# Moving normalisations, gate multiplies and residual adds from VectorE to GpSimd in a gated long-convolution block

## The chip, the cores and the metric

The kernel runs on one core of a Trainium2 chip. The core has five engines with a queue each: TensorE (PE in the profile; PEld is its weight load), VectorE (DVE), ScalarE (ACT), GpSimd (POOL) and SyncE (SP). Each engine works through its own queue in order, and semaphores hold an instruction until what it needs is done. The metric is the device time of one execution in microseconds; a version is judged by the median of its runs.

## The reference

The input x has 2048 positions of 640 channels, in bfloat16. It is normalised per position, and two branches are multiplied and added to it:

```python
xn = _layernorm(x, axis=-1)
# branch s: a 4-tap shift filter over k, times v, then a causal convolution
# of length 2048 per channel (by FFT of length 4096), plus a direct term, times xn
kv = k_shift * v
y = irfft(rfft(kv_pad) * rfft(kf_pad))[:S] + kv * ssm_D
s = xn * y
# branch g: a two-layer network on xn
g = _silu(_gelu(xn @ w1 + b1) @ w2 + b2)
return x + s * g
```

The hidden layer of the network is 1728 wide.

## The kernel before, in words

**Tiling.** 128 partitions hold 16 positions each, so a "row" n2 (0 to 15) is a tile of 128 x 640. Four rows make a chunk; the input lies in four tiles `xn_tiles`, one for each chunk c (0 to 3; the text counts chunks 1 to 4). A tile holds first x, then the normalised x, then that times the gate, and for the last chunk also the result.

**The network.** For each chunk: statistics (`ln_stats`, steps `ls`), the reciprocal root of the variance on GpSimd (`ln_eps`, `ln_root`; `lv`, `lr`), the normalisation of one row (`ln_norm`, `ln4` to `ln15`, line 361; the first chunk is normalised in the prologue by other code), transposes on TensorE (`tt`) and their copies to SBUF (`te`), the first layer (`h` on TensorE, line 377; `he` on ScalarE, line 383), the second layer by halves of a row (`g0` to `g31`, line 396), its silu on ScalarE into a buffer `sl` (`ge0` to `ge31`, line 401), and the multiplication of that into the normalised row (`ffn2_mul`, `gm0` to `gm31`, line 406). Chunk c has gates 8c to 8c + 7. The `sl` buffers are two: a silu can start only when the gate multiply of the buffer's last user is done. The second layer's PSUM tiles are two as well (`ps_ffn`).

**The convolution.** It is done as matrix multiplications in two factors. The filter: transposes (`kt`, `kc`), first factor (`kf`, evacuated by `ke` on ScalarE when the step ends in `.a`, on VectorE for `.d`), stores to a scratch in DRAM (`ks`, issued by GpSimd, line 437), reloads (`fl`), second factor (`ff`, `fe`). The input: shift filter and product on VectorE (`cv`, lines 467 to 473), first factor (`uf`, `ue`), stores by GpSimd (`us`, line 447), reloads issued by SyncE (`ml`, line 513), second factor (`mu`, line 521), products with the filter (`mp`, line 526), first inverse factor (`mc`, `me`), stores by GpSimd (`ms`, line 541), reloads (`yl`, line 547). A reload of either scratch takes one line out of every store, so it needs all sixteen stores. The stores' SBUF source is a ring of four pairs of rows (`pools["ring"]`). The PSUM tiles of this branch are three (`ps_big`).

**The end.** The second inverse factor (`inv2`, steps `y`, lines 553 and 554) gives a row in PSUM; `gate` (`yt`, line 560) multiplies it with the gated row. For the first three chunks the product goes to one of two `row` buffers `t1`; `out_add` (`yo`, line 564) adds the input to it and writes half of a pair `o` in a ring of two pairs (`pools["store"]`); when both rows of a pair are there, GpSimd issues its store (`out_store`, `ys`, line 568). The input is loaded a second time by chunks (`xq_load`, steps `q0` to `q3`, line 544) into two `quad` buffers, so the load for chunk 3 waits until the adds of chunk 1 are done, and that for chunk 4 until those of chunk 2 are done. For the last chunk the order is other: product first, then gate (`gm24` to `gm31`), then the add (`last_add`, `ga`, line 411) and the store by SyncE (`last_store`, `gs`).

**The order.** It is written out by hand in `PLAN`, a list of steps which the kernel issues one by one; each engine gets its instructions in this order. So an instruction that moves to another engine keeps its place in `PLAN` and takes the corresponding place in that engine's queue, between what the plan has before and after it there. GpSimd's queue before holds a few constants, three `lr`, and the stores `ks`, `us`, `ms` and `ys`.

Of the kernel before, what the change touches and what calls it, by code (L numbers as in the profile page):

```python
# [14 lines left out]
ALU = mybir.AluOpType  # L15
# [59 lines left out]
def kernel(  # L75
# [15 lines left out]
    nc = tc.nc  # L91

    CH = 4
# [218 lines left out]
    live = {}  # L312
    pools = {}

    def take(key, pool, shape, dtype, tag, bufs=None):
        if key not in live:
            live[key] = pool.tile(shape, dtype, tag=tag, name="%s%d" % key, **({"bufs": bufs} if bufs else {}))
        return live[key]
# [39 lines left out]
    def ln_norm(i):  # L358
        c, j = divmod(i, CH)
        xr = xn_tiles[c][:, j, :]  # L360
        nc.vector.tensor_scalar(out=xr, in0=xr, scalar1=live["mv", c][:, j, 0:1], scalar2=live["rs", c][:, j:j + 1],
                                op0=ALU.subtract, op1=ALU.mult)

    def x_tr(i):
# [21 lines left out]
    def ffn2_at(i):  # L386
        c, r = divmod(i, 2 * CH)
        q, h = divmod(r, 2)
        return c, q, slice(h * HALF, (h + 1) * HALF)
# [13 lines left out]
    def ffn2_mul(i):  # L403
        c, q, hs = ffn2_at(i)
        xr = xn_tiles[c][:, q, hs]
        nc.vector.tensor_tensor(out=xr, in0=xr, in1=live["sl", i][:], op=ALU.mult)  # L406

    def last_add(i):
        c, q, hs = ffn2_at(i)
# [151 lines left out]

    def out_add(n2):
        o_sb = take(("o", n2 // 2), pools["store"], None, None, None)
        nc.vector.tensor_tensor(out=o_sb[:, n2 % 2, :], in0=live["t1", n2][:], in1=live["xq", n2 // CH][:, n2 % CH, :],
                                op=ALU.add)

    def out_store(i):
        nc.gpsimd.dma_start(out=out_v[:, 2 * i:2 * i + 2, :], in_=live["o", i])
# [1 line left out]
    def prologue():  # L570
# [89 lines left out]
    steps = {  # L660
        "P": load_params, "pt": param_tr, "pb": param_out, "X": load_x, "A": load_w1, "B": load_w2, "C": load_kf, "K": load_k, "V": load_v,
        "ls": ln_stats, "lv": ln_eps, "lr": ln_root, "ln": ln_norm, "tt": x_tr, "te": x_tr_out,
        "h": ffn1, "he": ffn1_out, "g": ffn2, "ge": ffn2_silu, "gm": ffn2_mul, "ga": last_add, "gs": last_store,
        "w": f1_phase, "ws": f1_sines, "d": add_d, "em": tap3, "ee": tap3_out,
        "sp": small_iotas, "s": small_phase, "ss": small_sine, "sm": small_mats,
        "kt": k_tr, "kc": k_tr_out, "kf": k_f1, "ke": k_f1_out, "ks": k_store,
        "cv": kv_step, "uf": u_f1, "ue": u_f1_out, "us": u_store,
        "fl": kin_load, "ff": k_f2, "fe": k_f2_out, "it": i2_tr, "ie": i2_out,
        "ml": uin_load, "mk": swap_load, "mu": u_f2, "mp": product, "mc": inv1, "me": inv1_out, "ms": c_store,
        "q": xq_load, "yl": cab_load, "y": inv2, "yt": gate, "yo": out_add, "ys": out_store,  # L670
    }
    with tc.manual_schedule():
        prologue()
        for step in PLAN.split():
            kind, at, eng = re.fullmatch(r"([A-Za-z]+)(\d*)(?:\.(\w))?", step).groups()
# [31 lines left out]
```

## Time and profile before

| | us |
|---|---|
| median of 3 runs | 229.04 |
| lowest and highest run | 227.22, 229.06 |
| span of the profiled execution | 225.2 |
| median less that span | 3.84 |
| busy, TensorE / VectorE / ScalarE / GpSimd | 209.3 / 183.2 / 149.7 / 42.5 |

The profile gives the profiled execution's own time as its span, from the first instruction to the last; what lies around the span in that execution it doesn't give, and the timed runs stand 2.0 to 3.9 us above it. Rows of the timeline begin with the start and the duration in us, then engine, line, operation, output and inputs, and how many were merged; in brackets stands the idle time of the engine before it and what ended it. Rows by line give the number of instructions, the busy time in us and the mean of one in ns. Rows of the chain give the start, the length on the chain, and what it was. Rows by stage give each engine's busy time between two moments.

### The profile page before, as it was taken

To read this page: it belongs to the slowest core of one execution; us is meant where nothing else is said; L and a number is where in the kernel's file an instruction comes from. 1 tells how busy PE (TensorE), PEld (TensorE's weight loads), DVE (VectorE), ACT (ScalarE), POOL (GpSimd) and SP (SyncE) were. 2 spreads that over 40 slices of the span, in tenths; PEclk is the share of its full clock that TensorE was granted. 3 is DMA by queue.
4 is the path that set the end of the run, shared out by engine and by line. 5 is a ranking of instruction groups with operands and counts; after the bars stand their busy time and mean duration, and the time that the engine had idled before them with its cause. 6 is when DMAs were issued, how large, how long until landed. Compare 5 with 4: busy or idle time off the path is not lost.

```text
span 225.2 us, 3912 instructions
## 1 busy us (share of the span) xinstructions
PE 209.3 (93%) x1420; PEld 131.5 (58%) x1420; DVE 183.2 (81%) x309; ACT 149.7 (66%) x232; POOL 42.5 (19%) x72
## 2 busy tenths in 40 slices
PE   7869989899999899979999988999999999999993
PEld 4624457677555556645765544565777755457771
DVE  7799999989989999999859998999996125445792
ACT  3946697998988999999549665576762263671111
POOL 8000011032232345030200221203222000100010
PEclk9999999999999999999999999999999999999999
DMA  6999996645844469599849999866833694389223
GB/s 215 347 381 357 406 410 277 218 193 198 303 186 189 178 209 388 185 320 324 320 167 286 335 399 361 273 231 254 273 118 140 215 367 153 119 260 388 80 92 116
DMA packets 25209, 57.61 MB, mean 256 GB/s; under 512 B 2854, under 2 KB 14055, under 8 KB 25190
## 3 DMA queue, kind: packets, MB, share of 16 engines
q1 hardware_dynamic: 20726, 39.66, 50.7%
q0 software_dynamic: 4320, 17.70, 20.6%
q8 instruction: 11, 0.18, 0.3%
q14 instruction: 8, 0.07, 0.1%
q10 hardware_dynamic: 144, 0.01, 0.0%
HBM read 33.76 MB, written 18.35 MB: 231 GB/s over the span
## 4 chain that ended last, share of the span: by engine, by line
PE 59%; issue 13%; ACT 11%; DVE 7%; DMA 7%; SPq 1%; POOL 1%; DVEq 0%; POOLq 0%; ACTq 0%
PE g L396 20%; PE h L377 20%; ACT Khat L135 5%; DMA prm<-in_B_b_dram 4%; PE uf L337 3%; PE mc L534 2%; DMA scrC<-c 2%; PE mc L535 2%; PE kf L337 2%; PE mu L337 2%; PE y L553 2%; PE y L554 2%; DVE p L526 2%; DVE Khat L136 2%; PE ff L337 1%
## 5 line engine op out<-in xcount | busy, mean ns | idle before, releaser
L377 PE MATMUL h<-xnT,w_sb 128*128 128x512 bf16 x280 | 65.8, 379 | 1.3 <-ACT hT L383 1.0
L396 PE MATMUL g<-w_sb,hT 128*128 128x320 bf16 x448 | 63.7, 299 | 0.6 <-ACT sl L401 0.6
L396 PEld LDWEIGHTS <-hT 128*128 128x128 bf16 x448 | 43.8, 98 | 18.1 <-issue 0.8
L383 ACT ACTIVATE hT<-h,b_f 128x512 bf16<-128x512 f32 (+1 forms) x56 | 38.3, 690 | 23.2 <-PE h L377 20.7
L526 DVE TENSOR_TENSOR p<-mu,Khat 128x1280 bf16<-128x1280 f32 x32 | 45.8, 1484 | 3.1 <-PE mu L337 2.1
L377 PEld LDWEIGHTS <-w_sb 128*128 128x128 bf16 x280 | 27.3, 98 | 29.3 <-issue 1.5
L401 ACT ACTIVATE sl<-g 128x320 bf16<-128x320 f32 x32 | 14.0, 439 | 36.1 <-PE g L396 32.5
L135 ACT CAST c<-mc 128x640 bf16<-128x640 f32 x29 | 19.9, 692 | 6.5 <-PE mc L535 5.7
L541 POOL DMA_DIRECT2D scrC<-c x16 | 11.5, 718 | 51.9 <-ACT c L135 47.7
L406 DVE TENSOR_TENSOR xn<-xn,sl 128x320 bf16<-128x320 bf16 x32 | 10.0, 320 | 13.7 <-ACT sl L401 13.5
L469 DVE TENSOR_TENSOR uc<-uc,kvtmp 128x1280 bf16<-128x1280 bf16 x24 | 19.8, 824 | 0.7
L473 DVE TENSOR_TENSOR kvtmp<-kh,w_exp 128x1280 bf16<-128x1280 bf16 x24 | 19.7, 819 | 0.5
L534 PE MATMUL mc<-p,mats 128*128 128x320 bf16 x64 | 18.1, 298 | 1.6 <-DVE p L526 1.1
L560 DVE TENSOR_TENSOR t<-y,xn 128x640 bf16<-128x640 f32 x12 | 9.8, 820 | 10.6 <-PE y L554 10.5
L337 PEld LDWEIGHTS <-mats 128*128 128x128 bf16 x128 | 12.0, 97 | 10.8 <-issue 3.8
L535 PE MATMUL mc<-p,mats 128*128 128x320 bf16 x64 | 18.1, 298 | 0.0
L135 ACT CAST Khat<-uf 128x640 bf16<-128x640 f32 x26 | 17.0, 697 | 0.4 <-PE uf L337 0.4
L135 ACT CAST Khat<-ff 128x640 bf16<-128x640 f32 x24 | 15.5, 699 | 0.5 <-PE ff L337 0.4
L135 ACT CAST Khat<-kf 128x640 bf16<-128x640 f32 x22 | 15.1, 711 | 0.3 <-PE kf L337 0.2
L437 POOL DMA_DIRECT2D scrK<-Khat x16 | 8.9, 554 | 29.7 <-ACT Khat L135 16.6
L337 PE MATMUL mu<-kh,mats 128*128 128x320 bf16 x64 | 13.6, 298 | 0.8 <-DMA kh<-scrU 0.4
L337 PE MATMUL ff<-kin,mats 128*128 128x320 bf16 x64 | 12.3, 298 | 1.3 <-ACT Khat L135 1.3
(111 smaller groups left out, 269.0 us busy)
## 6 DMA issues: line engine op xcount, KB each, us to landing
scrK<-Khat POOLq DMA_DIRECT2D x16, 320.0 KB, 2.5
scrU<-Khat POOLq DMA_DIRECT2D x16, 320.0 KB, 4.3
kin<-scrK SPq DMA_DIRECT2D x16, 320.0 KB, 4.9
Khat<-Khat SPq DMA_DIRECT2D x32, 160.0 KB, 3.8
kh<-scrU SPq DMA_DIRECT2D x16, 320.0 KB, 5.2
scrC<-c POOLq DMA_DIRECT2D x16, 320.0 KB, 3.6
kh<-scrC SPq DMA_DIRECT2D x16, 320.0 KB, 6.0
kh<-in_A_k_dram SPq DMA_DIRECT2D x4, 640.0 KB, 5.9
```

What stands on the lines that cost most here:

```text
L135: return nc.scalar.copy(out=out_ap, in_=in_ap)
L337: nc.tensor.matmul(out=ps[:, h, 0:HALF], lhsT=lhsT, rhs=rhs[:, h * HALF:(h + 1) * HALF], start=start, stop=stop)
L377: nc.tensor.matmul(out=ps[:, :], lhsT=w1_sb[:, t, ft * P:(ft + 1) * P], rhs=xnT[:, t, :], start=(t == 0), stop=(t == DT - 1))
L383: nc.scalar.activation(out=hT[0:M, ft, :], in_=live["h", i][0:M, :], func=ACT.Gelu_apprx_tanh, bias=b1_f[0:M, ft:ft + 1], scale=1.0)
L396: nc.tensor.matmul(out=ps[:, 0:HALF], lhsT=hT[0:M, ft, q * P:(q + 1) * P], rhs=w2_sb[0:M, ft, hs], start=(ft == 0), stop=(ft == FT - 1))
L401: nc.scalar.activation(out=sl[:], in_=live["g", i][:, 0:HALF], func=ACT.Silu)
L469: nc.vector.tensor_tensor(out=uc[:], in0=uc[:], in1=kvtmp[:], op=ALU.add)
L473: nc.vector.tensor_tensor(out=(kvtmp if s else uc)[:], in0=kh[:, r0:r0 + KC, :], in1=w_exp[:, j:j + 1, :].to_broadcast([P, KC, D]), op=ALU ...
L526: nc.vector.tensor_tensor(out=p[:].rearrange("p k (h c) -> p k h c", h=2), in0=live["mu", g][:, None, :, 0:HALF].to_broadcast([P, 2, 2, HA ...
L534: nc.tensor.matmul(out=psC[:, h, 0:HALF], lhsT=I1a, rhs=p[:, 0, hs], start=True, stop=False)
L535: nc.tensor.matmul(out=psC[:, h, 0:HALF], lhsT=I1b, rhs=p[:, 1, hs], start=False, stop=True)
L541: nc.gpsimd.dma_start(out=pair_view(scrC)[g2], in_=live["c", g2][:])
```

## The change

Three operations are issued on GpSimd instead of VectorE: the normalisation of the rows of chunks 2 to 4 (twelve instructions of 128 x 640), the gate multiplies of chunks 1 to 3 (24 of the 32, of 128 x 320), and the addition of the input for rows 0 to 7 (eight of 128 x 640; the rows 8 to 11 stay, and so do the last chunk's own adds). `PLAN`, the buffers and everything else stay as they are.

```diff
     def ln_norm(i):
         c, j = divmod(i, CH)
         xr = xn_tiles[c][:, j, :]
-        nc.vector.tensor_scalar(out=xr, in0=xr, scalar1=live["mv", c][:, j, 0:1], scalar2=live["rs", c][:, j:j + 1],
+        nc.gpsimd.tensor_scalar(out=xr, in0=xr, scalar1=live["mv", c][:, j, 0:1], scalar2=live["rs", c][:, j:j + 1],
                                 op0=ALU.subtract, op1=ALU.mult)
...
     def ffn2_mul(i):
         c, q, hs = ffn2_at(i)
         xr = xn_tiles[c][:, q, hs]
-        nc.vector.tensor_tensor(out=xr, in0=xr, in1=live["sl", i][:], op=ALU.mult)
+        eng = nc.gpsimd if i < 24 else nc.vector
+        eng.tensor_tensor(out=xr, in0=xr, in1=live["sl", i][:], op=ALU.mult)
...
     def out_add(n2):
         o_sb = take(("o", n2 // 2), pools["store"], None, None, None)
-        nc.vector.tensor_tensor(out=o_sb[:, n2 % 2, :], in0=live["t1", n2][:], in1=live["xq", n2 // CH][:, n2 % CH, :],
-                                op=ALU.add)
+        eng = nc.gpsimd if n2 < 8 else nc.vector
+        eng.tensor_tensor(out=o_sb[:, n2 % 2, :], in0=live["t1", n2][:], in1=live["xq", n2 // CH][:, n2 % CH, :],
+                          op=ALU.add)
```

## The prediction

> **What bounds the kernel now.** I read the page first: busy shares, then the chain that ended last.
>
> ```profile
> span 225.2 us, 3912 instructions
> PE 209.3 (93%) x1420; PEld 131.5 (58%) x1420; DVE 183.2 (81%) x309; ACT 149.7 (66%) x232; POOL 42.5 (19%) x72
> PE 59%; issue 13%; ACT 11%; DVE 7%; DMA 7%; SPq 1%; POOL 1%; DVEq 0%; POOLq 0%; ACTq 0%
> ```
>
> TensorE is busy for 93% of the span and holds 59% of the chain; VectorE, busy for 81%, holds 7%. So VectorE's work is full of pieces that end while TensorE or ScalarE is later still, and taking work off VectorE is worth only what lies in those 7%. Then I read the busy time by stage, from the start of chunk 2's normalisation to the end of chunk 2's gates, the stretch in which most of the moved work lies:
>
> ```profile
> core 0: us, PE busy (x) PEld busy (x) DVE busy (x) ACT busy (x) POOL busy (x), PEclk, DMA share, GB/s
> 28.00:118.00 90.00, 84.61 (x617) 55.96 (x615) 83.29 (x155) 78.24 (x124) 22.25 (x35) 1.00 0.70 254
> 183.00:214.00 31.00, 31.00 (x190) 18.46 (x189) 16.47 (x29) 13.65 (x20) 2.19 (x4) 1.00 0.61 217
> ```
>
> From 28 to 118 all three compute engines are nearly full (TensorE idle for 5.4 of 90 us, VectorE for 6.7), each in its fixed order: a delay on any of them reaches the others. From 183 to 214 TensorE has no idle time at all, so nothing there can be won, only lost.
>
> **What moves, and its price.** Rows by line and form:
>
> ```profile
> L406 DVE TENSOR_TENSOR xn<-xn,sl 128x320 bf16<-128x320 bf16 x32 | 10.0, 320 | 13.7 <-ACT sl L401 13.5
> L361 DVE TENSOR_SCALAR xn<-xn,mv,rs 128x640 bf16<-128x640 bf16 x12 | 4.9, 439 | 0.0
> L564 DVE TENSOR_TENSOR w_exp<-t,xq 128x640 bf16<-128x640 bf16 x12 | 5.6, 490 | 2.5 <-DMA xq<-in_A_q_dram 2.2
> L356 POOL TENSOR_TENSOR rs<-ve,mhalf 128x4 f32<-128x4 f32 x3 | 4.5, 1513 | 28.4 <-DVE ve L352 28.4
> masks.py:199 POOL TENSOR_SCALAR_AFFINE_SELECT ident<-ident 128x128 bf16<-128x128 bf16 x1 | 0.3, 295 | 0.1
> L230 POOL IOTA GB<- 128x128 f32 x1 | 0.2, 243 | 0.0
> L229 POOL IOTA GB<- 128x16 f32 x1 | 0.1, 145 | 0.0
> ```
>
> VectorE gives up 24 of the 32 gate multiplies (24 x 0.320 = 7.7 us), 12 normalisations (12 x 0.439 = 5.3) and 8 of the 12 final adds counted here (8 x 0.490 = 3.9). What each costs on GpSimd no row shows. From below: no faster than on VectorE (0.32, 0.44, 0.49); nothing excludes that. From above: the only GpSimd row that reads two tensors takes 1.51 us, a power on 4 elements; I use it as a high end of 1.5 for a multiply and, with the per-element part below, 2.9 for an add. Between them, by the small GpSimd rows: two iotas differ by 112 elements and 98 ns, 0.875 ns per element written and 131 ns fixed; the select reads and writes 128 elements in 295 ns, (295 - 131) / 128 = 1.28 ns; a second operand, taken at the cost of one more pass, makes 2.16 ns. So a normalisation is 0.131 + 640 x 1.28 ns = 0.95 us, a gate multiply 0.131 + 320 x 2.16 ns = 0.82, an add 0.131 + 640 x 2.16 ns = 1.51. These estimates I take, being from rows with real streaming in them.
>
> [...]
>
> **Loss A: the first stores (43 to 49 us).** GpSimd also issues the stores of the first transform, in plan order `ke1.d ks0 gm2 ge4 ln6 kf3 ke3.d ks1 kf4 ke4.a gm4 ge5`. The silu outputs have two buffers, held by the second and third gates, so ge4 must wait for gm2 and ge5 for gm4.
>
> ```profile
> 43.83 0.32 DVE L406 TENSOR_TENSOR xn<-xn,sl 128x320 bf16<-128x320 bf16 x1
> 44.06 0.44 DVE L361 TENSOR_SCALAR xn<-xn,mv,rs 128x640 bf16<-128x640 bf16 x1
> 45.18 0.32 DVE L406 TENSOR_TENSOR xn<-xn,sl 128x320 bf16<-128x320 bf16 x1
> 44.53 0.73 POOL L437 DMA_DIRECT2D scrK<-Khat  x1 [10.00 <-DVE xn L361]
> 45.83 0.55 POOL L437 DMA_DIRECT2D scrK<-Khat  x1 [0.57 <-ACT Khat L135]
> 44.68 0.46 ACT L401 ACTIVATE sl<-g 128x320 bf16<-128x320 f32 x1
> 45.59 0.48 ACT L401 ACTIVATE sl<-g 128x320 bf16<-128x320 f32 x1
> 44.80 0.34 ACT sl L401
> 45.73 0.34 ACT sl L401
> ```
>
> Now gm2 (43.83) runs beside the store; afterwards it stands behind it. Store to 45.26, gm2 to 46.08, ge4 at 46.1 instead of 44.68; ln6 to 47.03, the second store (0.55) to 47.58, gm4 to 48.4, ge5 at 48.4 instead of 45.59: 2.8 us. If the first store starts as soon as its data is there, some 0.6 earlier, it is 2.2; I take 2.5. The last two rows are from the chain: both silus stand on it, and behind them in ScalarE's order stand the evacuations for which TensorE waits, so nothing hides this. The transposes of chunk 2 (TensorE at 45.6) wait for ln6 too, but less. Lower end 1.4 (VectorE's durations), upper end 5. The three normalisations and two gates before 43 us come no later than now: GpSimd is idle from 34.5 to 44.5.
>
> **Loss B: the last scratch store (110 us).** gm12 and gm10 stand on GpSimd ahead of the last two stores of the input's transform; the reload waits for all of them.
>
> ```profile
> 109.77 0.54 POOL L447 DMA_DIRECT2D scrU<-Khat  x1 [0.74 <-ACT Khat L135]
> 114.53 0.88 SPq L513 DMA_DIRECT2D kh<-scrU  x2
> 117.50 0.43 PE L337 MATMUL mu<-kh,mats 128*128 128x320 bf16 x2
> ```
>
> The store before it, at 108.49, is pushed to 109.0 by gm12, and gm10 (0.82) puts the last at 110.4: 0.6 late, and the reload (114.53) and the matmul (117.50) with it. Between 0.1 and 2. The eight normalisations of chunks 3 and 4 delay two earlier stores (87 to 91 us) by about 2 us each, but all reloads wait for the last store, and the store ring is four pairs deep: nothing. ln14, ln15 and gm13 to gm15 sit in front of stores that come 1.5 us or more later: nothing.
>
> **Loss C: the final adds (186 to 222 us).** TensorE has no slack here, and now each half pair of output rows takes GpSimd 1.51 instead of 0.49, with the stores in the same queue.
>
> ```profile
> 192.89 0.56 POOL L568 DMA_DIRECT2D out_dram<-w_exp  x1 [0.70 <-DVE w_exp L564]
> out_dram<-w_exp POOLq DMA_DIRECT2D x6, 320.0 KB, 2.7
> 197.28 0.89 DVE L564 TENSOR_TENSOR w_exp<-t,xq 128x640 bf16<-128x640 bf16 x2
> 198.74 0.38 SPq L544 DMA_DIRECT2D xq<-in_A_q_dram  x1
> 206.84 0.49 DVE L564 TENSOR_TENSOR w_exp<-t,xq 128x640 bf16<-128x640 bf16 x1 [2.21 <-DMA xq<-in_A_q_dram]
> 211.39 2.33 DVE L560 TENSOR_TENSOR xn<-y,xn 128x640 bf16<-128x640 f32 x3
> 213.60 7.79 PE L396 MATMUL g<-w_sb,hT 128*128 128x320 bf16 x56
> ```
>
> yo4 and yo5 run from 190.5 to 193.5, the first store goes out by 194.1, yo1 ends at 195.6, and its store, now at 192.89, starts at 195.6 and lands 2.7 later, at 198.3. The store buffer has two pairs, so yo2 and yo3 (197.28) wait for that landing: 198.4 to 201.4, not 198.17. They free the buffer into which chunk 3's input is loaded (198.74); the load goes 3.2 late, and VectorE, which already sat 2.2 us for it before 206.84, gets to yo8 at 210.1. Its idle time and the next gate's (1.1 us) give some back: the three gate products at 211.39 start at 213.15. The three rotating PSUM buffers wait for those products, so y9 and y10 hold TensorE, and the last 56 matmuls (213.60) start at 215.3: 1.7 late, and the end with them. With VectorE's durations 0; with 2.9 us an add about 9.
>
> **Gains.** Of the VectorE pieces taken away, these stand on the chain:
>
> ```profile
> 71.05 0.23 DVE xn L406
> 106.09 0.16 DVE xn L406
> 107.71 0.08 DVE xn L406
> 107.86 0.32 DVE xn L406
> ```
>
> 0.23 + 0.16 + 0.08 + 0.32 = 0.8 us. The other 20 gates, the adds and the normalisations (which come well ahead of their transposes) lie where ScalarE or TensorE ends later. The last four gates and adds stay on VectorE.
>
> **Sum.** 2.5 + 0.6 + 1.7 - 0.8 = +4.0, on a span of 225.2: 229.2. The median of the runs, 229.04, lies 3.84 above that span; what lies around the span is untouched, so 233.0.
>
> **Rivals.**
>
> First, *the two engines block each other*. In 28 to 118 GpSimd gets 16 gates and 12 normalisations, 16 x 0.82 + 12 x 0.95 = 24.5 us, beside a VectorE that spends its time largely on multiplies and adds of two tensors:
>
> ```profile
> L469 DVE TENSOR_TENSOR uc<-uc,kvtmp 128x1280 bf16<-128x1280 bf16 x24 | 19.8, 824 | 0.7
> L473 DVE TENSOR_TENSOR kvtmp<-kh,w_exp 128x1280 bf16<-128x1280 bf16 x24 | 19.7, 819 | 0.5
> 32.98 1.55 POOL L356 TENSOR_TENSOR rs<-ve,mhalf 128x4 f32<-128x4 f32 x1 [26.80 <-DVE ve L352]
> 33.66 0.82 DVE L469 TENSOR_TENSOR uc<-uc,kvtmp 128x1280 bf16<-128x1280 bf16 x1
> ```
>
> These two rows are 39.5 us of the 89 from 15 to 104, 44%, so 10.8 us of the new GpSimd work would meet one. If one engine stands still meanwhile, and half falls on each, VectorE loses 5.4 of the 28 pieces' gain (16 x 0.23, the spacing from 43.83 to 44.06, + 12 x 0.44 = 9.0) and GpSimd's queue is later by 0.2 a piece, which adds about 0.6 to loss A and takes the 0.8 away: 234.4. If all falls on VectorE, it is 1.8 us worse off in a stretch where it has 6.7 idle, with waits spread all over: up to 237 or 238. I price it at 236. Against it: the power (32.98 to 34.53) ran beside a two-tensor add that took its usual 0.82; but it streams 4 elements only, so the row proves little.
>
> [...]
>
> Second, the other side, *VectorE's relief sets the pace: faster*. If VectorE's fullness is what holds TensorE from 28 to 118, the 9.0 us fill TensorE's 5.4 idle. It decides if GpSimd's gate is short enough to hand back the silu buffer (below about 0.4 us); then loss A is under 1.4 and loss C nothing: 229.0 - 5.4 + 1.4 + 0.1 = 225.1 at best, more likely 226. Against it: only 7% of the chain is VectorE.
>
> Third, *hidden anyway*: the evacuations catch up after 50 us and the store to yo2 lands sooner: only 0.6 + 1 remain against 0.8, 229.8.
>
> **How the numbers follow.** One per cent, 2.3 us, is about what a measurement of this kernel can tell from no change. Forecast (231.4 to 235) 0.40; blocking (234.4 to 240) 0.28; adds near their high price (240 or more) 0.08; hidden 0.16; faster 0.08. Same takes the hidden case, 0.16, slower 0.40 + 0.28 + 0.08 = 0.76. The range from 228.5 to 241 leaves out the faster case and the far end of the high price, which by the upper ends is 5 + 2 + 9 - 0.8, some 15 us.
>
> **What would show it.** Right: GpSimd rows of L361, L406 and L564 near 0.95, 0.82 and 1.51; ScalarE idle before L401 for gates on GpSimd near 45 and 48 us; yo8 on VectorE idle for xq by more than 2.2; TensorE idle before the last 56 matmuls. Blocking would show as L469 and L473 longer than 0.82, or GpSimd rows far above the estimates beside VectorE and not in the quiet stretch from 171 to 183. I am wrong if GpSimd's rows are under 0.5, or if ge4 and ge5 start on time.

## The result and the profile after

The changed kernel takes 246.57 us (median of four runs, 246.37 to 248.06), the kernel before in the same comparison 228.13 (226.75 to 229.06): a ratio of 1.084, with an interval of 1.076 to 1.091. It is slower, as predicted, but by 18 us instead of 4; 246.6 lies above the predicted range.

The page of the changed kernel, in the parts that answer to those of before:

```profile
span 244.5 us, 3921 instructions
PE 212.6 (87%) x1407; PEld 133.5 (55%) x1420; DVE 175.2 (72%) x265; ACT 149.9 (61%) x232; POOL 106.9 (44%) x116
PE 58%; DVE 17%; DMA 6%; POOL 6%; ACT 5%; issue 5%; SPq 1%; DVEq 0%; ACTq 0%; POOLq 0%
```

TensorE does the same work in a longer span (93% to 87%). VectorE is less busy than before but holds 17% of the chain instead of 7%, and GpSimd is on it.

To see where the 19.3 us of span came from I cut both executions at four marks: the first filter transpose `kt`, the last first-factor matmul of the filter `kf`, the first second-factor matmul of the input `mu`, and the first output matmul `y`. By tile, the rows give the first and the last start of each, before:

```profile
L421 PE MATMUL kt<-ident,Khat x80: 216/225/233, 41.0 to 75.0; 128*128 128x128 bf16 x80
L337 PE MATMUL kf<-kT,WA x32: 296/299/309, 42.4 to 76.0; 128*128 128x320 bf16 x32
L337 PE MATMUL mu<-kh,mats x64: 296/299/309, 117.5 to 166.5; 128*128 128x320 bf16 x64
L553 PE MATMUL y<-kh,GA x32: 298/299/300, 184.3 to 213.3; 128*128 128x320 bf16 x32
```

and after:

```profile
L422 PE MATMUL kt<-ident,Khat x80: 216/226/314, 41.1 to 82.6; 128*128 128x128 bf16 x80
L337 PE MATMUL kf<-kT,WA x32: 296/299/471, 42.4 to 83.6; 128*128 128x320 bf16 x32
L337 PE MATMUL mu<-kh,mats x64: 296/299/310, 135.3 to 185.5; 128*128 128x320 bf16 x64
L554 PE MATMUL y<-kh,GA x32: 296/299/299, 203.3 to 232.6; 128*128 128x320 bf16 x32
```

Stage 1, from the first `kt` (41.0) to the last `kf` (76.0), took 35.0 us and now takes 83.6 - 41.1 = 42.5: **+7.5**. Stage 2, on to `mu`, took 41.5 and now 51.7: **+10.2**. Stage 3, to `y`, 66.8 and 68.0: **+1.2**. Stage 4, to the end of the span, 40.9 and 41.2: **+0.3**. The predicted loss was 2.5, 0.6, nothing and 1.7 in these stages. Counting from the first `kt` leaves out the start, which differs from one profiled execution to the next: the first `kt` comes between 41.0 and 44.1 us in the kernels below. Each kernel was profiled in one execution only, so the figures by stage are those of one execution.

The moved operations, rows by line (busy us and mean ns of one):

```profile
L361 POOL TENSOR_SCALAR xn<-xn,mv,rs 128x640 bf16<-128x640 bf16 x12 | 33.3, 2776 | 0.3
L407 POOL TENSOR_TENSOR xn<-xn,sl 128x320 bf16<-128x320 bf16 x24 | 19.9, 830 | 40.4 <-ACT sl L401 40.2
L566 POOL TENSOR_TENSOR w_exp<-t,xq 128x640 bf16<-128x640 bf16 x8 | 11.0, 1394 | 8.1 <-DVE t L561 5.5 <-DMA out_dram<-w_exp 2.6
L470 DVE TENSOR_TENSOR uc<-uc,kvtmp 128x1280 bf16<-128x1280 bf16 x24 | 23.3, 971 | 0.7
L474 DVE TENSOR_TENSOR kvtmp<-kh,w_exp 128x1280 bf16<-128x1280 bf16 x24 | 20.6, 860 | 0.5
```

A gate takes 0.83 us and an add 1.39, close to the estimates (0.82 and 1.51). A normalisation takes **2.78 us, against an estimate of 0.95**. Where this bites is in GpSimd's timeline, first around 40 us and then around 100:

```profile
35.60 1.63 POOL L356 TENSOR_TENSOR rs<-ve,mhalf 128x4 f32<-128x4 f32 x1
37.34 9.10 POOL L361 TENSOR_SCALAR xn<-xn,mv,rs 128x640 bf16<-128x640 bf16 x3
46.38 0.77 POOL L438 DMA_DIRECT2D scrK<-Khat  x1
47.19 0.80 POOL L407 TENSOR_TENSOR xn<-xn,sl 128x320 bf16<-128x320 bf16 x1
47.96 2.50 POOL L361 TENSOR_SCALAR xn<-xn,mv,rs 128x640 bf16<-128x640 bf16 x1
50.42 0.61 POOL L438 DMA_DIRECT2D scrK<-Khat  x1
51.06 0.80 POOL L407 TENSOR_TENSOR xn<-xn,sl 128x320 bf16<-128x320 bf16 x1
...
95.02 5.49 POOL L361 TENSOR_SCALAR xn<-xn,mv,rs 128x640 bf16<-128x640 bf16 x2
100.46 0.62 POOL L448 DMA_DIRECT2D scrU<-Khat  x1
101.13 8.69 POOL L361 TENSOR_SCALAR xn<-xn,mv,rs 128x640 bf16<-128x640 bf16 x3
109.78 0.60 POOL L448 DMA_DIRECT2D scrU<-Khat  x1
110.43 2.50 POOL L361 TENSOR_SCALAR xn<-xn,mv,rs 128x640 bf16<-128x640 bf16 x1
112.90 0.78 POOL L407 TENSOR_TENSOR xn<-xn,sl 128x320 bf16<-128x320 bf16 x1
```

The gate in the last row is `gm9`. Six normalisations (5.49 + 8.69 + 2.50 = 16.7 us) and two stores stand ahead of it in GpSimd's queue. It holds one of the two `sl` buffers, so the silu `ge11` waits for it, and behind `ge11` stands everything else that ScalarE has to do. The same place on ScalarE and on TensorE:

```profile
113.71 0.44 ACT L401 ACTIVATE sl<-g 128x320 bf16<-128x320 f32 x1 [10.33 <-POOL xn L407]
```
```profile
114.78 0.69 PE L337 MATMUL uf<-uc,WB 128*128 128x320 bf16 x2 [9.98 <-ACT Khat L135]
```

ScalarE stands still for 10.3 us and TensorE for 10.0, about as long as stage 2's loss of 10.2. Around 48 us the same happens on a smaller scale: `ge4` and `ge5` wait 3.15 and 2.85 us for the gates at 47.19 and 51.06. By stage, the clock that TensorE was granted (the column after POOL's) fell with the stalls:

```profile
47.00:58.00 11.00, 6.74 (x46) 4.79 (x46) 4.31 (x5) 6.00 (x12) 6.76 (x8) 0.69 0.24 94
110.00:115.00 5.00, 0.22 (x1) 0.10 (x1) 0.00 (x0) 1.29 (x3) 4.18 (x4) 0.50 0.21 82
115.00:120.00 5.00, 5.00 (x22) 2.81 (x21) 1.72 (x3) 4.63 (x9) 2.18 (x4) 0.51 0.74 231
120.00:125.00 5.00, 4.58 (x32) 2.92 (x30) 4.39 (x6) 4.36 (x9) 0.45 (x1) 1.00 0.95 331
```

From 115 to 120 TensorE is busy all the time and gets 22 matmuls done where the next 5 us have 32. Four matmuls of 128 x 320 that start at 115.38 take 1.22 us, four that started at 103.82, before the stall, took 0.71.

### The profile page after: what moved, and what is told of

Same layout as the page of the kernel before. It is cut to its first block, busy times and chain, and to the rows that moved or that the text cites. A ratio compares the mean times of both kernels' runs of the same rounds, so it can differ in the third digit from the quotient of the medians.

```text
span 244.5 us, 3921 instructions
## 1 busy us (share of the span) xinstructions
PE 212.6 (87%) x1407; PEld 133.5 (55%) x1420; DVE 175.2 (72%) x265; ACT 149.9 (61%) x232; POOL 106.9 (44%) x116
## 4 chain that ended last, share of the span: by engine, by line
PE 58%; DVE 17%; DMA 6%; POOL 6%; ACT 5%; issue 5%; SPq 1%; DVEq 0%; ACTq 0%; POOLq 0%
PE g L396 20%; PE h L377 14%; POOL xn L361 4%; PE uf L337 4%; DVE kvtmp L474 3%; PE kf L337 3%; ACT Khat L135 3%; DVE uc L470 3%; DMA scrC<-c 3%; PE ff L337 2%; DMA kh<-scrU 2%; PE mc L535 2%; PE mc L536 2%; PE y L554 2%; PE y L555 2%
## 5 line engine op out<-in xcount | busy, mean ns | idle before, releaser
L377 PE MATMUL h<-xnT,w_sb 128*128 128x512 bf16 x267 | 64.0, 379 | 2.0 <-ACT hT L383 1.1
L407 POOL TENSOR_TENSOR xn<-xn,sl 128x320 bf16<-128x320 bf16 x24 | 19.9, 830 | 40.4 <-ACT sl L401 40.2
L361 POOL TENSOR_SCALAR xn<-xn,mv,rs 128x640 bf16<-128x640 bf16 x12 | 33.3, 2776 | 0.3
L470 DVE TENSOR_TENSOR uc<-uc,kvtmp 128x1280 bf16<-128x1280 bf16 x24 | 23.3, 971 | 0.7
L474 DVE TENSOR_TENSOR kvtmp<-kh,w_exp 128x1280 bf16<-128x1280 bf16 x24 | 20.6, 860 | 0.5
L337 PEld LDWEIGHTS <-mats 128*128 128x128 bf16 x128 | 12.5, 100 | 10.8 <-issue 4.2
L438 POOL DMA_DIRECT2D scrK<-Khat x16 | 9.1, 569 | 18.4 <-ACT Khat L135 15.4
L337 PE MATMUL uf<-uc,WB 128*128 128x320 bf16 x32 | 7.4, 329 | 10.6 <-ACT Khat L135 10.4
L136 DVE CAST Khat<-ff 128x640 bf16<-128x640 f32 x8 | 6.4, 820 | 12.6 <-PE ff L337 12.6
```

The source lines that it names most:

```text
L337: nc.tensor.matmul(out=ps[:, h, 0:HALF], lhsT=lhsT, rhs=rhs[:, h * HALF:(h + 1) * HALF], start=start, stop=stop)
L361: nc.gpsimd.tensor_scalar(out=xr, in0=xr, scalar1=live["mv", c][:, j, 0:1], scalar2=live["rs", c][:, j:j + 1], op0=ALU.subtract, op1=ALU.mult)
L377: nc.tensor.matmul(out=ps[:, :], lhsT=w1_sb[:, t, ft * P:(ft + 1) * P], rhs=xnT[:, t, :], start=(t == 0), stop=(t == DT - 1))
L407: eng.tensor_tensor(out=xr, in0=xr, in1=live["sl", i][:], op=ALU.mult)
L470: nc.vector.tensor_tensor(out=uc[:], in0=uc[:], in1=kvtmp[:], op=ALU.add)
L474: nc.vector.tensor_tensor(out=(kvtmp if s else uc)[:], in0=kh[:, r0:r0 + KC, :], in1=w_exp[:, j:j + 1, :].to_broadcast([P, KC, D]), op=ALU ...
```

## The experiments

The theory: the normalisation's price is the cause, through what stands behind it in GpSimd's queue (the gates that hold the silu buffers, and the stores). The rivals: the two engines block each other, or the three parts each cost something of their own. First the parts by themselves.

**Normalisations alone, gates alone, adds alone.** Each kernel undoes the other two parts of the change:

```diff
# normalisations alone: ffn2_mul and out_add
-        eng = nc.gpsimd if i < 24 else nc.vector
+        eng = nc.vector
-        eng = nc.gpsimd if n2 < 8 else nc.vector
+        eng = nc.vector
# gates alone, adds alone: ln_norm, and out_add or ffn2_mul
-        nc.gpsimd.tensor_scalar(out=xr, in0=xr, ...
+        nc.vector.tensor_scalar(out=xr, in0=xr, ...
```

> Only the twelve normalisations on GpSimd. Theory (price and place: a normalisation costs GpSimd 2.5 to 3.0 us, and what stands behind it in GpSimd's queue waits): no silu waits for GpSimd any more, so the 10 us stall of ScalarE before gate 11 is gone; what remains is the first store and the transposes of chunk 2 behind ln7, ln5, ln4 and ln6 (about +4) and the stores behind six normalisations in a row (0 to +6): ratio 1.02 to 1.045. Rival (the engines block each other): most of the meeting work is here, so most of the loss stays: ratio 1.05 to 1.08, with the VectorE adds and multiplies of 128 x 1280 longer all over.

> Only the gate multiplies of chunks 1 to 3 on GpSimd, 0.8 us each. Price and place: gates wait behind one or two stores of 0.55, so the two silus near 45 us start about 1 to 2.5 us late, less up to 0.8 us of relief on VectorE: ratio 1.00 to 1.01. Blocking: 16 gates beside VectorE's two-tensor work, 0.5 us each: ratio 1.02 to 1.03.

> Only the adds of rows 0 to 7 on GpSimd, 1.4 us each. The trace of the changed kernel shifts by only 0.3 us over this stage: ratio 0.998 to 1.004. The prediction's loss C says +1.7 us: ratio 1.0075.

Normalisations alone: 238.89 us, a ratio of 1.0485 (1.0417 to 1.0553); gates alone: 231.19, 1.0171 (1.0098 to 1.0244); adds alone: 227.64, 0.9999 (0.9956 to 1.0042). In stages, by the same four marks, normalisations cost +4.0, +5.9, +0.1, -0.1, gates +2.2, +1.0, +0.3, +0.2, adds nothing over 0.2 anywhere. The normalisations are the dearest part, but the three sum to 9.9 + 3.7 + 0.4 = 14.0 of 19.2: about 5 us (about 4 by the medians) arise only when the parts are together. The 10 us wait of `ge11` is such a piece: it needs a gate with normalisations ahead of it in one queue. The times of the first two kernels lie between what the theory expected and what blocking would give, so by themselves they decide little. VectorE's products of 128 x 1280 (L470 and L474, 824 and 819 ns in the kernel before) were held up in both, with means of 948 and 839 ns beside the gates and 877 and 916 beside the normalisations; beside the adds they weren't (824 and 820). With gates alone, ScalarE's rows are the prediction's loss A:

```profile
46.84 0.44 ACT L401 ACTIVATE sl<-g 128x320 bf16<-128x320 f32 x1 [1.70 <-POOL xn L407]
48.19 0.44 ACT L401 ACTIVATE sl<-g 128x320 bf16<-128x320 f32 x1 [0.33 <-POOL xn L407]
```

With adds alone the mechanism of loss C is there too, but costs nothing; GpSimd's, SyncE's and VectorE's rows:

```profile
199.48 2.73 POOL L566 TENSOR_TENSOR w_exp<-t,xq 128x640 bf16<-128x640 bf16 x2 [2.53 <-DMA out_dram<-w_exp]
...
202.24 0.33 SPq L545 DMA_DIRECT2D xq<-in_A_q_dram  x1
...
208.70 0.49 DVE L566 TENSOR_TENSOR w_exp<-t,xq 128x640 bf16<-128x640 bf16 x1 [3.35 <-DMA out_dram<-w_exp]
```

`yo2` waits for the store's landing until 199.48 (198.4 was foretold), and the load of chunk 3's input goes out at 202.24, 3.5 us late (3.2 was foretold). But it has landed within 6.5 us where before it took 8.1 (198.74 to 206.84); what comes last before `yo8` is now, by the third row, the landing of `yo2`'s and `yo3`'s own store. `yo8` starts at 208.70, 1.9 later than before, 0.6 of which is this execution's later start of the outputs (first `y` at 184.9 instead of 184.3). The slack before the last gates takes the remaining 1.3.

**All but the normalisations.**

```diff
-        nc.gpsimd.tensor_scalar(out=xr, in0=xr, ...
+        nc.vector.tensor_scalar(out=xr, in0=xr, ...
```

> The change without the normalisations: gates and adds on GpSimd. Price and place: the sum of the two parts, +0.5 to +3 us, ratio 1.00 to 1.013, so over 80% of the loss comes from the normalisations. Blocking: ratio 1.03 or more. The prediction's own sum with the normalisations at no cost would be about +3, 1.013.

233.06 us, 1.0230 (1.0154 to 1.0307), again between the two expectations; stages +2.0, +0.9, +0.6, +0.3. By stages gates and adds cost together what they cost apart (3.8 and 4.1 us). The time is that of the prediction, 233.0, but the loss isn't: it is 5.3 us above this comparison's kernel before (227.74), where the prediction added 4.0 to 229.04, normalisations included.

**Is it the silu buffer?** Three buffers instead of two; or `gm9` moved in the plan to directly behind `ge9`, ahead of four of the six normalisations (`ln13` and `ln9` still stand before it, so not ahead of five, as the expectation has it):

```diff
# a third buffer
-        sl = take(("sl", i), ffnp, [P, HALF], BF16, "sl", 2)
+        sl = take(("sl", i), ffnp, [P, HALF], BF16, "sl", 3)
# gm9 first
-... us6 fl5 g9 ge9 ff3
+... us6 fl5 g9 ge9 gm9 ff3
-... ff6 fe6.d gm9 ff9 ...
+... ff6 fe6.d ff9 ...
```

> The whole change with three silu buffers instead of two, nothing else. If the wait of silu 11 for gate 9's buffer is what stops ScalarE and TensorE for 10 us, a third buffer lets it run: the loss falls by 6 to 10 us, ratio 1.04 to 1.06, and the idle time before silu 11 is gone. If the stall has another cause (stores, transposes, blocking), the ratio stays at 1.075 or more.

> The whole change, with the step gm9 placed right behind ge9, ahead of five of the six normalisations, in the plan. The same wait undone by order, with two buffers as before: if place decides, the loss falls by 6 to 10 us, ratio 1.04 to 1.06, near that of three buffers. If the normalisations' own lateness (or the stores behind them) is the cause, the ratio stays at 1.07 or more.

Three buffers: 1.0616 (1.0486 to 1.0746), stages +6.9, +6.6, +0.7, +0.3. `gm9` first: 1.0682 (1.0603 to 1.0762), stages +7.8, +6.3, +0.4, +0.3. The 10 us wait for `gm9` is gone in both, yet both ratios lie above the 1.04 to 1.06 expected, and only some 4 of stage 2's 10.2 us come back: a second hold stands behind the first. ScalarE and TensorE with three buffers:

```profile
113.95 1.88 ACT L135 CAST Khat<-uf 128x640 bf16<-128x640 f32 x3 [5.16 <-DMA scrU<-Khat]
```
```profile
114.70 1.88 PE L337 MATMUL ff<-kin,mats 128*128 128x320 bf16 x6 [5.38 <-ACT Khat L135]
```

Now ScalarE waits for a slot of the store ring, because the stores that would free it stand behind the same normalisations. With `gm9` first this wait is 2.31 us, and TensorE waits 2.87 for VectorE's `uc` besides. The silu buffer is one exit of the jam, not its source.

**What does each form cost, and do the engines hold each other up?** A kernel of before with a tail: eight operations on GpSimd alone, four products of 128 x 1280 on VectorE alone, then the eight beside 24 such products.

```diff
+        g.tensor_scalar(out=o, in0=A, scalar1=sc, scalar2=s2, op0=ALU.subtract, op1=ALU.mult)   # twice
+        g.tensor_scalar(out=o, in0=A, scalar1=sc, scalar2=None, op0=ALU.mult)
+        g.tensor_scalar(out=o, in0=A, scalar1=0.5, scalar2=2.0, op0=ALU.subtract, op1=ALU.mult)
+        g.tensor_single_scalar(out=o, in_=A, scalar=2.0, op=ALU.mult)
+        g.tensor_copy(out=o, in_=A)
+        g.tensor_tensor(out=o, in0=A, in1=B2, op=ALU.mult)
+        g.tensor_tensor(out=o, in0=A, in1=sc.to_broadcast([P, D]), op=ALU.mult)
```

> The kernel before, with extra work behind its last step that belongs to nothing: eight GpSimd instructions on 128 x 640 bf16 with VectorE idle (normalisation's form twice, one operation by a per-partition scalar, two operations by constants, one by a constant, a copy, a product of two tensors, a product with a broadcast scalar), four VectorE products of 128 x 1280 with GpSimd idle, then both at once. Its time is longer by this work. Expected alone: the normalisation's form 2.5 us, the product of two tensors 1.37, a VectorE product 0.82. If it is the per-partition scalars that cost, the form with constants is near 1 us; if it is the second operation, the form with one is near 1.3. Both at once: if a whole instruction blocks, VectorE's products are longer by up to 2.5 us or GpSimd's by 0.8 each; if it is by pieces, both longer by 0.3 to 0.6.

This kernel was run once. GpSimd's timeline, alone from 222.96 us, when VectorE's last step of the kernel itself ends, up to 234 us, and then beside VectorE:

```profile
218.93 2.52 POOL L672 TENSOR_SCALAR w_sb<-w_sb,b_f 128x640 bf16<-128x640 bf16 x1
221.55 2.50 POOL L673 TENSOR_SCALAR w_sb<-w_sb,b_f 128x640 bf16<-128x640 bf16 x1
224.15 1.89 POOL L674 TENSOR_SCALAR w_sb<-w_sb,b_f 128x640 bf16<-128x640 bf16 x1
226.13 2.36 POOL L675 TENSOR_SCALAR w_sb<-w_sb 128x640 bf16<-128x640 bf16 x1
228.57 1.82 POOL L676 TENSOR_SCALAR w_sb<-w_sb 128x640 bf16<-128x640 bf16 x1
230.46 0.71 POOL L677 COPY w_sb<-w_sb 128x640 bf16<-128x640 bf16 x1
231.26 1.39 POOL L678 TENSOR_TENSOR w_sb<-w_sb 128x640 bf16<-128x640 bf16 x1
232.72 1.25 POOL L679 TENSOR_TENSOR w_sb<-w_sb,b_f 128x640 bf16<-128x640 bf16 x1
...
238.68 3.17 POOL L672 TENSOR_SCALAR w_sb<-w_sb,b_f 128x640 bf16<-128x640 bf16 x1
241.95 3.02 POOL L673 TENSOR_SCALAR w_sb<-w_sb,b_f 128x640 bf16<-128x640 bf16 x1
```

A normalisation's form (two operations, a scalar for each partition) takes 2.50 us, as it does at 110.43 us in the changed kernel, with VectorE, ScalarE and TensorE idle. One operation instead of two takes 1.89, constants instead of scalars in a tile save another 0.1, and a plain copy is 0.71. Neither of the two causes that the expectation names, the scalars for each partition or the second operation, explains it alone. So the price lies in the form with a scalar operand, and a product of two whole tensors (1.39) is cheaper than a product by one scalar (1.82). Beside VectorE's products the two normalisations took 3.17 and 3.02; VectorE's rows, alone and then beside GpSimd:

```profile
234.44 3.40 DVE L683 TENSOR_TENSOR w_sb<-w_sb 128x1280 bf16<-128x1280 bf16 x4
238.72 25.28 DVE L683 TENSOR_TENSOR w_sb<-w_sb 128x1280 bf16<-128x1280 bf16 x24 [0.88 <-POOL w_sb L688]
```

24 products alone would be 6 x 3.40 = 20.4, so the eight GpSimd operations cost VectorE 4.9 us, 0.6 each. There is contention, but small beside the 2.50.

**The whole change at the price that the prediction took.** The normalisation is replaced by an in-place copy on GpSimd; this kernel doesn't normalise chunks 2 to 4.

```diff
-        nc.gpsimd.tensor_scalar(out=xr, in0=xr, ...,
-                                op0=ALU.subtract, op1=ALU.mult)
+        nc.gpsimd.tensor_copy(out=xr, in_=xr)
```

> The whole change, but each of the twelve normalisations on GpSimd is a copy in place, 0.7 us alone and about 0.95 beside VectorE: the price that the prediction gave to a normalisation. (Left out: the normalisation of chunks 2 to 4.) Theory (the loss of 19 us is the price of 2.5 to 3.0 us a normalisation, and what stands behind them): all but the gates' loss goes, ratio 1.015 to 1.03, and no wait of 10 us before silu 11. Rival (place or mutual blocking counts, whatever the price): ratio 1.05 or more.

```profile
L361 POOL COPY xn<-xn 128x640 bf16<-128x640 bf16 x12 | 11.4, 977 | 0.0
```

A copy took 0.98 here, almost exactly the prediction's 0.95, and the time is 234.52 us, 1.0279 (1.0224 to 1.0335), as expected; stages +4.3, +1.0, +0.7, +0.3. The places in GpSimd's queue are those of the change. The copy reads no statistics, but the reciprocal root that a normalisation needs still stands ahead of it in the same queue, so what differs is the form of the operation and with it the duration. The kernel before in this comparison takes 227.49, so the loss is 7.0 us instead of 18.4: 11.4 are gone, and stage 2 falls from +10.2 to the +1.0 of gates alone. Blocking doesn't explain the difference: VectorE's products are held up here as in the changed kernel,

```profile
L469 DVE TENSOR_TENSOR uc<-uc,kvtmp 128x1280 bf16<-128x1280 bf16 x24 | 22.6, 942 | 0.7
L473 DVE TENSOR_TENSOR kvtmp<-kh,w_exp 128x1280 bf16<-128x1280 bf16 x24 | 21.2, 883 | 0.5
```

which is 24 x (0.118 + 0.064) = 4.4 us more than before, against 4.5 in the changed kernel.

**Order instead of price.** `gm9` behind `ge9`, and the first two of the last chunk's normalisations (`ln13`, `ln12`) behind `gm15`, so that four instead of six stand between 95 and 113 us:

```diff
-... g8 ge8 gm8 ln13 ln9 uf13 ... g9 ge9 ff3
+... g8 ge8 gm8 ln9 uf13 ... g9 ge9 gm9 ff3
-fe3.a ln12 ff1 ... ff6 fe6.d gm9 ff9
+fe3.a ff1 ... ff6 fe6.d ff9
-... g15 ge15 gm15 ff21
+... g15 ge15 gm15 ln12 ln13 ff21
```

> The whole change with the normalisations at full price but at other places of the plan: gm9 right behind ge9, and ln12 and ln13 (chunk 4, whose transposes come 50 us later) behind gm15 instead of ahead of the stores near 87 to 91 us. Theory (what stands behind the normalisations in GpSimd's queue pays): of the 10.2 us lost between the filter's last transform and the first reload 6 to 9 come back, ratio 1.04 to 1.05. Rival (the price is paid wherever they stand): 1.065 or more.

241.54 us, 1.0599 (1.0533 to 1.0664); stages +9.2, +3.7, +1.1, +0.3. In stage 2 the theory holds: 6.5 of 10.2 come back. The ratio missed its expectation, in part because of stage 1, where this kernel issues the same instructions as the changed one and yet lost 1.7 more in the profiled execution, the slowest of the four. Most of that lies in one group of 14 matmuls of the second layer, behind the stalls near 50 us. In this kernel:

```profile
56.14 3.94 PE L396 MATMUL g<-w_sb,hT 128*128 128x320 bf16 x14
```

and the same group in the changed kernel:

```profile
54.36 2.43 PE L396 MATMUL g<-w_sb,hT 128*128 128x320 bf16 x14
```

In the kernel before it takes 2.07, from 53.15. The granted clock was 0.50 from 56 to 60 us in this kernel, and 0.91 from 54.4 to 58.4 in the changed kernel. In these two executions the clock came back at different moments after the stalls: it was 0.99 from 60 to 64 us in this kernel, and 1.00 from 56 to 60 already in the changed kernel.

**Chunk 2's normalisations back on VectorE**, the rest of the change as it is:

```diff
-        nc.gpsimd.tensor_scalar(out=xr, in0=xr, ...
+        eng = nc.gpsimd if c > 1 else nc.vector
+        eng.tensor_scalar(out=xr, in0=xr, ...
```

> The whole change, but the four normalisations of chunk 2 (ln4 to ln7) stay on VectorE; the eight of chunks 3 and 4 stay on GpSimd. In the changed kernel 7.5 of the 19 us are lost between the first filter transpose and the last first-factor matmul of the filter, the stage of these four. Theory: with them gone that stage loses 2 us (as with the gates alone), the next still 10: ratio 1.055 to 1.065. Rival (that stage's loss is the gates behind the stores, or mutual blocking): the stage still loses 5 us or more, ratio 1.07 or more.

243.18 us, 1.0620 (1.0499 to 1.0741), within the expectation; stages +3.9, +10.6, +0.7, +0.2. Stage 2 keeps its whole loss, so that comes from the normalisations of chunks 3 and 4, and chunk 2's make some 3.6 of stage 1's 7.5. The stage was expected to fall to 2: gates alone issue the same in stage 1 and cost +2.2. But here the clock was again below 1 (0.68 from 48 to 52 us, 0.90 from 52 to 56), and there it wasn't. So a profiled stage 1 is certain to about 2 us only.

**Gates alone with three silu buffers** (the edits shown above, together):

> Only the gates on GpSimd, with three silu buffers. If the gates' loss (3.7 us from the first filter transpose to the end) is the silus' wait for their buffer behind the first stores, as loss A of the prediction has it, 2 us go: ratio 1.005 to 1.01. If it is VectorE's two-tensor work being held by GpSimd's, nothing goes: ratio 1.015 or more.

230.28 us, 1.0116 (1.0072 to 1.0160), between the two expectations; stages +0.9, +1.0, +0.5, +0.2. Of the gates' 2.2 us in stage 1, 1.3 are the silu buffer: the waits of `ge4` and `ge5` fall from 1.70 and 0.33 us to 0.75 for `ge5` alone. The rest stays without a single name; VectorE's two-tensor products beside GpSimd's gates, 1.30 instead of 0.82 us where they meet, are part of it.

**Only what lies in quiet stretches**: the last chunk's normalisations, `ln12` and `ln13` behind `gm15` as above, the gates of chunk 3, and the adds.

```diff
+        eng = nc.gpsimd if c == NCH - 1 else nc.vector
-        eng = nc.gpsimd if i < 24 else nc.vector
+        eng = nc.gpsimd if 16 <= i < 24 else nc.vector
```

> Only what nobody waits for on GpSimd: the normalisations of chunk 4 (ln12 and ln13 behind gm15 in the plan), the gates of chunk 3, the adds of rows 0 to 7; the rest on VectorE as before. Theory: no loss, and at most half a microsecond of relief for VectorE near 90 us: ratio 0.995 to 1.002. Rival (any sharing costs): 1.005 or more.

228.50 us, 1.0053 (1.0022 to 1.0085); stages +0.1, -0.1, +0.7, +0.2. VectorE is relieved of 4 normalisations, 8 gates and 8 adds (6.4 us busy less) and nothing is gained. The ratio lies above the theory's 0.995 to 1.002 and where its rival, any sharing costs, has it: about 1 us is lost, clear of noise. It isn't the products' hold, for L471 and L475 take 824 and 819 ns as before; its cause stays open. Even here a normalisation, from 131.12 to 133.57, stands in front of a store of the inverse. No version tried beats the kernel before.

## Why the prediction was wrong, point by point

**The step that failed is the price of a normalisation**: "a normalisation is 0.131 + 640 x 1.28 ns = 0.95 us". It is 2.50 alone and 2.78 in the kernel. The estimate took the rate of a select whose row shows no scalar operand. I gave high ends for the multiply (1.5) and the add (2.9), both far above what came, but none for the normalisation, the one operation whose form no row of GpSimd showed. With the copy at 0.98 in its place the kernel loses 7.0 us instead of 18.4, so the price is shown, not only argued, to carry some 11 of the 18 us. At the predicted price the loss is still 3 us more than the forecast 4.0.

**Two sentences fell with it.** "The three normalisations and two gates before 43 us come no later than now: GpSimd is idle from 34.5 to 44.5": the root ended at 37.23 instead of 34.53, the three ran until 46.4, and only then did the first store go out, at 46.38 instead of 44.53. "The eight normalisations of chunks 3 and 4 delay two earlier stores by about 2 us each ... nothing": they delayed the gate behind them, which the sentence doesn't name, and through the silu buffer all of ScalarE and TensorE for 10 us; and when that way out is opened, the store ring, which I had called deep enough, holds them for 5. At 0.98 the sentence holds (stage 2 +1.0, as without normalisations).

**Loss A, 2.5**: right in size for the gates (2.0 and 2.2 in the two kernels without moved normalisations), though its mechanism, the silu buffer, accounts for only 1.3 of the 2.2 and the sum had put one normalisation into it. It was enlarged to 7.5 by the normalisations ahead of the gates and, to an extent that differed between two profiled executions, by the clock (0.61 from 52 to 56 us and 1.00 from 56 to 60 in the changed kernel, 0.50 in both stretches in the one with the other order). **Loss B, 0.6**: with gates alone the last three stores start at 111.57, 112.91 and 114.25, a gate between each two, where before they started at 107.59, 108.49 and 109.77: from the first to the last 0.5 us more. Stage 2 lost 0.9 to 1.0 in the kernels without moved normalisations, within the bounds. **Loss C, 1.7**: oversized; it measured nothing. The wait of `yo2` was as foretold, and so was the late load, but it landed faster, `yo8` came 1.3 us late instead of 3.25, and that held no PSUM buffer long enough to stop TensorE. **Gains, 0.8**: none to be seen, nor with the late pieces alone. **The base**: 229.04 was the median of three runs, 3.84 above the profiled span, and the prediction took all of this for time around the span. Every run with a span of its own lies 1.7 to 2.2 above it; the rest was the difference between executions, and the kernel before takes 227.5 to 228.1 in the later comparisons. A base that was too high and the oversized C are why 233.0 meets the 233.06 of gates and adds: that is luck.

**The rivals.** *Blocking* was there, and on VectorE's rows in about the size it was given (5.4): L470 and L474 grew by 24 x (0.147 + 0.041) = 4.5 us, and a normalisation by 0.28. But the normalisation takes 2.50 with the other engines idle (at 110.43 us in the changed kernel), and the products grew as much with the copies, so blocking isn't the main cause. What it costs in time beside the gates, as a part of the losses above that have no name, wasn't separated. *VectorE's relief* named as its condition a gate below about 0.4 us; a gate takes 0.83, and no version that relieves VectorE is faster, the late pieces neither. *Hidden anyway* is true of the adds alone.

## What to carry to other kernels

Before an operation moves to another engine, find a row of exactly its form on that engine, or measure it alone; here the neighbouring form gave 0.95 us where the operation took 2.50 alone and 2.78 in the kernel, and without such a row the high end must be as wide as for the other terms. The price of the slow operation was paid here by what stood behind it in GpSimd's queue (16.7 us of normalisations ahead of `gm9`, and ScalarE stood still for 10.3): list, for each run of moved operations, every store and every buffer release behind it, and add up the whole run, not one operation. Here an engine that was 81% busy but held 7% of the chain had nothing to give.

## What the runs showed of the hardware

GpSimd's operation with a scalar operand took 2.50 us on 128 x 640 bf16 (1.82 to 1.89 with one operation), more than its product of two tensors (1.39), while VectorE does the normalisation in 0.44. In the changed kernel GpSimd took 1.39 for an add against VectorE's 0.49 and 0.83 for a gate against 0.32: 2.6 to 2.8 times as long with two tensors, where the normalisation alone took 5.7 times as long. A copy took GpSimd 0.71 alone.

VectorE's two-tensor products and GpSimd held each other up by about half a microsecond for each GpSimd operation: 4.9 us on VectorE's side for eight, and on GpSimd's 0.65 and 0.52 for the two normalisations. If the eight, 14.4 us alone, had taken turns with 20.4 us of products, the two together would have needed 34.8 us; VectorE was through in 25.3. So no hold over the whole operation is to be seen.

TensorE's granted clock was 1.00 throughout before. In the 10 us stall of the changed kernel it fell to 0.50 near 110 us, some 5 us after TensorE's last matmuls before the stall (104.36), and it stayed at 0.50 and 0.51 until 120 us, some 5 us after TensorE had resumed at 114.78. That the clock accounts for all of the 1.7 us that the same instructions lost more in one execution than in another wasn't shown, nor what sets the moment at which it comes back.
